# Values loaded two tokens per partition for four chunks, keys in even-odd order, and another opening order, in an attention and SwiGLU kernel

## The chip, the cores and the metric

The kernel runs on one core of a Trainium2 chip. The metric is the device time of one execution in microseconds; before and after are compared by the median of several runs. One execution of the kernel before was also recorded by the hardware profiler. Its engines are TensorE (PE, with its weight loads shown as PEld), VectorE (DVE), ScalarE (ACT), GpSimd (POOL) and SyncE (SP), which here only issues DMAs.

## What is computed

A causal attention with a window of 64 keys over 8 sequences of 576 tokens with 8 heads of 64, and behind it a feed-forward block with a gate, over all 4608 tokens. Inputs and outputs are fp32; the kernel multiplies in bf16.

```python
def _attn_ref(q, k, v):                       # each [8, 8, 576, 64]
    scores = scale * np.matmul(q, k.transpose(0, 1, 3, 2))
    rel = pos[:, None] - pos[None, :]
    mask = (rel >= 0) & (rel < window)        # window = 64
    scores = np.where(mask, scores, -1000000000.0)
    attn = np.exp(scores - np.max(scores, axis=-1, keepdims=True))
    attn = attn / (np.sum(attn, axis=-1, keepdims=True) + 1e-09)
    return np.matmul(attn, v)

def _moe_ref(x, w_gate, w_val, w_out):        # x [4608, 512], d_ff 1536
    g = x @ w_gate
    silu = g * (1.0 / (1.0 + np.exp(-g)))
    return silu * (x @ w_val) @ w_out
```

## The kernel before

The tokens are cut into 36 groups of 128 (`ORDER`): four groups for the first 512 tokens of each sequence, and four that hold the last 64 tokens of two sequences each. Two groups make a chunk (n = 0 to 17, groups 2n and 2n+1), four make a tile t of 512 tokens for the feed-forward block.

For each chunk, keys and queries are loaded as fp32 (`load`, two neighbouring tokens to a partition, so that a run in memory is 512 bytes; or `load1`, one token to a partition, runs of 256 bytes), cast to bf16 (`cast_k`) and turned so that the head dimension lies on the partitions: by TensorE against an identity and a copy out of PSUM (`turn2`), or by DMA (`turn1`). `turn2` undoes the two-token layout in its copy. `keys_before` copies the last 64 keys of a chunk to the next one's ring. Values are loaded by group, one token to a partition (`load_vg`), and `cast_v` writes them three times as bf16: `vo`, the group as it is, and the two halves to `ve`, which holds the same values shifted by 64 tokens, so that each block of 64 queries meets its 128 keys in one tile (`vL` keeps what the last 64 tokens of a sequence need).

For each group, `scores` multiplies keys and queries into two PSUM tiles. With `masked` it first writes a large negative number where the window doesn't reach (matmuls of `minus` with the identity); without, `weigh` multiplies by a mask of 0 and 1 on DVE after ACT's exponential. `products` multiplies by the values with a column of ones, `norm` divides by the sum of that column on DVE (four instructions), and `turn_x` (TensorE, then a copy on ACT) or `turn_x1` (DMA) puts the result into `xT` of its tile.

The feed-forward block of tile t is 12 `step(t, m)`, each with four matmuls for the gate, four for the values (0.86 us each four) and a tanh on ACT, then `finish` with two DVE instructions, and four `project(t, s)` of 12 matmuls. A step may be cut by columns (`step(0, 11, 0, 256)`). Weights come as 12 loads of 512 KB (`weights(s, i)`, chunk s serves steps 2s and 2s+1, i is gate or values) and six for the output (`weights_o`), each with a cast (`cast_w`, `casts_o`). `warm(n)` is n matmuls on zeros that compute nothing.

Every engine takes its instructions in the order in which the code is written (`manual_schedule`), and SP issues all DMAs in that order, each behind the release of the buffer that it fills. PSUM has four tiles (`ps_a`, tag a) for scores, products, turns and projections, and two each for gate and values (`ps_f`). `stage` holds two fp32 chunks each of keys, queries and values, `wst` six weight loads.

From line 386 to line 637 an opening is written out by hand: attention of groups 0 to 11, the 24 steps of tiles 0 and 1, the four projections of tile 0, all weights, and what the loop needs at its start. From line 641 the loop repeats a fixed pattern for each two groups, with three steps to a group; it takes up work that the opening left ready. The change touches `load_vg`, `turn2`, `cast_v`, `weigh` and `begin`, and writes the opening anew.

Of the kernel before, what the change touches and what calls it, by code (L numbers as in the profile page):

```python
# [17 lines left out]
def kernel(  # L18
# [17 lines left out]
    ORDER += [(7, i) for i in range(4)] + [(4, None), (6, None)]  # L36
    VW = 65
    KR, VR, ER, QR = 3, 5, 3, 3
    NEG = -1e30

    ctx.enter_context(tc.manual_schedule())
# [24 lines left out]

    Es = [cst.tile([P, H, 2, 64], BF16, name=f"E{i}") for i in range(ER)]

    masks = [cst.tile([P, 2, 64], BF16, name=f"mask{i}") for i in range(2)]

    minus = [cst.tile([P, P], BF16, name=f"minus{i}") for i in range(2)]
    identb = cst.tile([P, P], BF16, name="identb")
# [31 lines left out]
    def load_vg(g):  # L104

        if g % 2 == 0:
            staged["v_f", g // 2] = stage.tile([P, 2, H, D], FP32, name="v_f", tag="v_f")[:]
        for y, b, s in tokens(g):
            m = y.stop - y.start
            sp.dma_start(  # L110
                staged["v_f", g // 2][y, g % 2],
                v[b, :, s:s + m, :].rearrange("h r d -> r h d"))

    words = {}

# [41 lines left out]
    def turn2(n, nm, eng):  # L157

        x_b = words.pop((nm, n))
        o = 64 if nm == "k_f" else 0  # L160
        ring = kT[n % KR] if nm == "k_f" else qT[n % QR]
        engs = eng if isinstance(eng, tuple) else (eng,)
        m = 4 // len(engs)
        tps = []
        for i in range(len(engs)):
            tp = ps_a.tile([P, m, 2, P], BF16, name="tp", tag="a")
            for c in range(2):
                for p in range(m):
                    a = P * (m * i + p)
                    nc.tensor.transpose(tp[:, p, c], x_b[:, c, a:a + P], identb[:])  # L170
            tps.append(tp)
        for i, tp in enumerate(tps):
            y = ring[:, m * i:m * i + m, o:o + 256].rearrange("r p (x c) -> r p x c", c=2)
            copy(engs[i], y, tp[:].rearrange("r p c x -> r p x c"))

    def cast_v(g, engs):

        engs = engs if isinstance(engs, tuple) else (engs,) * 3
        x = staged["v_f", g // 2][:, g % 2]
        lo, hi = slice(0, 64), slice(64, P)  # L180
        b, i = ORDER[g]
        z = vo[g % VR]
        if i is None:
            to = (vL[hi, b], lo), (vL[hi, b + 1], hi)
        else:
            copy(engs[0], z[:, :, 0:D], x)
            to = (ve[g % VR][hi], lo), (vL[lo, b] if i == 3 else ve[(g + 1) % VR][lo], hi)
        for e, (y, a) in zip(engs[1:], to):
            if e is None:
                dve.tensor_copy(y[:, :, 0:D], z[a][:, :, 0:D])  # L190
            else:
                copy(e, y[:, :, 0:D], x[a])
# [34 lines left out]

    def weigh(g):
        E = Es[g % ER]
        mk = masks[1 if ORDER[g][1] == 0 else 0]  # L230
        ps, masked = sps.pop(g)
        for a, x in enumerate(ps):
            e = E[:, a:H:2]
            act.activation(e, x[:], AF.Exp, scale=0.125)  # L234
            if not masked:
                dve.tensor_mul(e, e, mk[:].unsqueeze(1).to_broadcast([P, 4, 2, 64]))  # L236
# [57 lines left out]
    def cast_w(s, i, eng):  # L294
        copy(eng, (wg, wv)[i][:, :, 256 * s:256 * s + 256], raw.pop((i, s))[:])
# [50 lines left out]
        for _ in range(n):  # L346
            nc.tensor.matmul(w_ps[:], wz[:, 0:P], wz[:])

    def begin():

        dve.memset(wz[:], 0.0)
# [11 lines left out]
        for a in range(2):  # L363

            y = minus[0][64 * a:64 * a + 64]
            pool.affine_select(
                out=y, in_=y, compare_op=ALU.is_ge, fill=NEG,
                base=64, pattern=[[-1, P]], channel_multiplier=1,
            )
            pool.affine_select(  # L370
                out=y, in_=y, compare_op=ALU.is_ge, fill=NEG,
                base=-1, pattern=[[1, P]], channel_multiplier=-1,
            )

        pool.tensor_copy(minus[1][:, 64:P], minus[0][:, 64:P])
# [9 lines left out]

    begin()
    load(0, k, "k_f")
    load(0, q, "q_f")
    load(1, k, "k_f")
    load_vg(0)  # L390
    cast_k(0, "q_f", (dve, act))
    cast_k(0, "k_f", pool)
    warm(11)
    turn2(0, "k_f", (act, dve))
    load(1, q, "q_f")
    warm(3)
    turn2(0, "q_f", (act, dve))
    warm(3)
    scores(0, True)
    scores(1)  # L400
    load_vg(1)
    cast_k(1, "k_f", (act, dve))
    cast_v(0, (pool, act, dve))
    load_vg(2)
    load_vg(3)
    cast_v(1, pool)
    weigh(1)
    weights(5, 0)
    weigh(0)
    warm(7)  # L410
    turn2(1, "k_f", act)
    weights(5, 1)
    cast_k(1, "q_f", dve)
    keys_before(1)
    turn2(1, "q_f", act)
    products(0)
    norm(0)
    cast_v(2, (pool, pool, act))
    warm(4)
    products(1)  # L420
    scores(2, True)
    norm(1)
    weights(0, 0)
    weights(0, 1)
    load(2, k, "k_f")
    scores(3, True)
    cast_v(3, (pool, dve, act))
    load(2, q, "q_f")
    weigh(2)
    weigh(3)  # L430
    turn_x(0)
    cast_w(5, 0, pool)
    warm(1)
    products(2)
    warm(2)
    products(3)
    norm(2)
    norm(3)
    turn_x(1)
    turn_x(2)  # L440
    load_vg(4)
    load_vg(5)
    cast_w(5, 1, pool)
    warm(2)
    step(0, 11, 0, 256)
    finish()
    cast_w(0, 0, pool)
    cast_w(0, 1, dve)
    turn_x(3)
    keys_before(2)  # L450
    step(0, 10, 0, 256)
    finish()
    cast_k(2, "k_f", (dve, pool))
    step(0, 10, 256, 256)
    finish()
    weights(4, 0)
    step(0, 0)
    weights(4, 1)
    load(3, k, "k_f")
    cast_k(2, "q_f", (act, dve))  # L460
    turn2(2, "k_f", (dve, act))
    turn2(2, "q_f", (dve, act))
    step(0, 11, 256, 256)
    finish()
    keys_before(3)
    cast_v(4, (pool, pool, act))
    scores(5, True)
    cast_v(5, (pool, dve, act))
    load(3, q, "q_f")
    weigh(5)  # L470
    scores(4, True)
    weigh(4)
    cast_w(4, 0, pool)
    finish()
    step(0, 1)
    products(5)
    load_vg(6)
    cast_w(4, 1, act)
    products(4)
    norm(5)  # L480
    weights(2, 0)
    step(0, 8)
    norm(4)
    cast_k(3, "k_f", (act, dve))
    turn_x(4)
    turn_x(5)
    finish()
    cast_k(3, "q_f", pool)
    turn2(3, "k_f", act)
    step(0, 9)  # L490
    finish()
    turn2(3, "q_f", (dve, act))
    weights(2, 1)
    load_vg(7)
    finish()
    weights(1, 0)
    step(1, 8, 0, 256)
    scores(7, True)
    finish()
    cast_w(2, 0, act)  # L500
    weights(1, 1)
    scores(6, True)
    cast_v(6, pool)
    weigh(7)
    cast_w(2, 1, dve)
    step(1, 10, 0, 256)
    load(4, q, "q_f")
    step(0, 4)
    finish()
    weigh(6)  # L510
    step(1, 4, 0, 256)
    cast_v(7, pool)
    products(7)
    finish()
    products(6)
    cast_w(1, 0, act)
    step(1, 11, 0, 256)
    load(4, k, "k_f")
    load_vg(8)
    finish()  # L520
    norm(6)
    cast_k(4, "q_f", pool)
    cast_w(1, 1, act)
    cast_k(4, "k_f", pool)
    cast_v(8, pool)
    finish()
    step(0, 5)
    step(0, 3)
    weights(3, 1)
    norm(7)  # L530
    turn_x(6)
    cast_w(3, 1, pool)
    finish()
    turn_x(7)
    turn2(4, "q_f", (dve, act))
    weights(3, 0)
    step(0, 2)
    keys_before(4)
    weights_o(4)
    finish()  # L540
    turn2(4, "k_f", act)
    finish()
    step(1, 2)
    finish()
    scores(8)
    load(5, k, "k_f")
    weigh(8)
    scores(9)
    weights_o(5)
    step(1, 8, 256, 128)  # L550
    load(5, q, "q_f")
    load_vg(9)
    cast_w(3, 0, pool)
    finish()
    cast_k(5, "k_f", pool)
    step(1, 5)
    step(0, 7)
    finish()
    finish()
    weigh(9)  # L560
    step(1, 7)
    finish()
    casts_o(5, pool)
    keys_before(5)
    turn2(5, "k_f", act)
    keys_before(6)
    step(0, 6)
    cast_k(5, "q_f", act)
    cast_v(9, pool)
    finish()  # L570
    step(1, 6)
    weights_o(2)
    finish()
    weights_o(3)
    products(8)
    casts_o(3, pool)
    products(9)
    load_vg(10)
    weights_o(0)
    step(1, 10, 256, 256)  # L580
    norm(8)
    load_vg(11)
    casts_o(2, pool)
    finish()
    casts_o(4, pool)
    cast_v(10, pool)
    step(1, 3)
    norm(9)
    turn2(5, "q_f", act)
    finish()  # L590
    turn_x(8)
    weights_o(1)
    load1(6, k, "k_f")
    casts_o(0, dve)
    casts_o(1, pool)
    step(1, 0)
    scores(10)
    scores(11)
    weigh(10)
    weigh(11)  # L600
    load1(7, k, "k_f")
    load1(7, q, "q_f")
    step(1, 9)
    cast_v(11, (dve, pool, pool))
    finish()
    turn_x(9)
    project(0, 0)
    load(6, q, "q_f")
    load_vg(12)
    project(0, 2)  # L610
    step(1, 4, 256, 256)
    products(11)
    products(10)
    cast_k(7, "k_f", (act, pool))
    finish()
    cast_k(6, "k_f", (dve, pool))
    norm(11)
    finish()
    turn1(6, "k_f")
    step(1, 1)  # L620
    cast_k(6, "q_f", act)
    norm(10)
    load_vg(14)
    cast_v(12, (act, None, None))
    keys_before(7)
    turn1(7, "k_f")
    finish()
    project(0, 1)
    turn_x(10)
    step(1, 8, 384, 128)  # L630
    load1(8, k, "k_f")
    turn_x(11)
    finish()
    project(0, 3)
    step(1, 11, 256, 256)
    load_vg(13)
    turn2(6, "q_f", (dve, act))


    dve.memset(vL[:, :, :, D:VW], 1.0)  # L640
    for w in range(8, NG, 2):
        t, s = divmod(w, 4)
        n = w // 2
# [87 lines left out]
```

The softmax here doesn't subtract the row's maximum and nothing guards it: scores larger than these inputs give would overflow.

## Time and profile before

| | us |
|---|---|
| median of 5 runs | 338.34 (337.71 to 338.69) |
| the profiled execution, its own time | 338.61 |
| its span | 336.9 |
| first matmul of the loop, from the span's start | 87.17 |
| loads of values, 256 KB each, issue to landing (median) | 5.2 |
| loads of keys and queries, 512 KB each | 7.1 |
| loads of gate and value weights, 512 KB each | 6.5 and 6.8 |

The span runs from the program's first instruction to its last; the time of an execution contains some 1.7 us around it. A row of the profile names the line of the kernel, the engine, the operation, what it writes and reads, and its shape; "idle before" is how long the engine waited ahead of it and on what.

### The profile page before, as it was taken

Reading aid. Unit: us, or ns where it says so; the run is one execution under the profiler, and the core shown is the slowest. Engines: PE = TensorE matmul, PEld = TensorE weight load, DVE = VectorE, ACT = ScalarE, POOL = GpSimd, SP = SyncE. Lnnn points to the kernel's source line nnn. Section 1 sums busy time; section 2 is a strip of 40 time slices with the busy share of each in tenths; the row PEclk is TensorE's granted clock in tenths of the full one; section 3 lists DMA queues with packets and bytes.
Section 4 is the critical chain, followed back from the end, with each engine's and each line's share of the span. In section 5 each row is a group of like instructions: output and inputs, shape, how many; then the busy total and the mean of one; then the engine's idle time right before and its main releaser. Section 6 shows DMA issues by size and latency. Waiting matters only on the chain.

```text
span 336.9 us, 7160 instructions
## 1 busy us (share of the span) xinstructions
PE 324.9 (96%) x2690; PEld 163.5 (49%) x2731; DVE 228.3 (68%) x491; ACT 151.9 (45%) x268; POOL 100.5 (30%) x148
## 2 busy tenths in 40 slices
PE   7888999999999999999999999999998999999996
PEld 3455665545544444444444444444444444444444
DVE  4667998895687767777768675867675866655520
ACT  3858876566525252525253434343433334233222
POOL 4543455751143333333333333223333110000000
DMA  7999999979978889898989689889787430211013
GB/s 204 265 312 279 309 287 324 315 161 238 190 141 174 169 163 183 166 181 174 171 179 165 149 163 177 170 173 188 140 193 124 108 65 34 63 31 31 33 47 109
DMA packets 150610, 56.83 MB, mean 169 GB/s; under 512 B 124720, under 2 KB 144560, under 8 KB 150576
## 3 DMA queue, kind: packets, MB, share of 16 engines
q1 hardware_dynamic: 150576, 56.38, 77.2%
q8 instruction: 21, 0.34, 0.4%
q14 instruction: 13, 0.11, 0.1%
HBM read 37.75 MB, written 9.44 MB: 140 GB/s over the span
## 4 chain that ended last, share of the span: by engine, by line
PE 83%; DMA 8%; DVE 4%; ACT 2%; issue 1%; SPq 1%; DVEq 0%; ACTq 0%
PE o_ps L334 26%; PE g_ps L316 25%; PE v_ps L316 24%; DMA q_f<-in_q_dram 3%; PE ao_ps L252 3%; PE s_ps L221 2%; DMA kT<-k_fb 2%; DMA v_f<-in_v_dram 2%; PE tp L170 1%; DVE sg L327 1%; ACT E L234 1%; SPq L89 1%; DVE hT L328 1%; DVE x_b L263 1%; DMA out_dram<-os__4900 1%
## 5 line engine op out<-in xcount | busy, mean ns | idle before, releaser
L316 PE MATMUL g_ps<-xT,wg 128*128 128x512 bf16 (+2 forms) x426 | 110.4, 366 | 3.7 <-DVE sg L327 1.9
L316 PE MATMUL v_ps<-xT,wv 128*128 128x512 bf16 (+1 forms) x457 | 111.6, 366 | 0.5 <-POOL wv L120 0.2
L327 DVE SCALAR_TENSOR_TENSOR sg<-th,g_ps 128x512 f32<-128x512 f32 (+1 forms) x115 | 74.9, 652 | 50.2 <-ACT th L321 50.0
L321 ACT ACTIVATE th<-g_ps 128x512 f32<-128x512 f32 (+1 forms) x115 | 65.8, 572 | 78.3 <-PE g_ps L316 75.7
L334 PE MATMUL o_ps<-wo,hT 128*128 128x512 bf16 (+2 forms) x454 | 98.4, 368 | 0.2
L328 DVE TENSOR_TENSOR hT<-sg,v_ps 128x512 bf16<-128x512 f32 (+1 forms) x115 | 75.4, 655 | 11.9 <-PE xtp L276 0.5
L316 PEld LDWEIGHTS <-wv 128*128 128x128 bf16 x460 | 44.6, 98 | 49.5 <-ACT wv L118 0.7
L334 PEld LDWEIGHTS <-hT 128*128 128x128 bf16 x456 | 43.6, 98 | 49.5
L316 PEld LDWEIGHTS <-wg 128*128 128x128 bf16 x460 | 41.9, 98 | 44.0 <-issue 2.2
L234 ACT ACTIVATE E<-s_ps 128x512 bf16<-128x512 f32 x72 | 38.6, 596 | 8.1 <-PE s_ps L221 8.0
L120 POOL CAST k_fb<-k_f 128x1024 bf16<-128x1024 f32 (+1 forms) x16 | 16.0, 1006 | 59.6 <-DMA k_f<-in_k_dram 45.1
L263 DVE TENSOR_TENSOR x_b<-ao_ps,r 128x256 bf16<-128x256 f32 x72 | 30.6, 425 | 2.5
L120 POOL CAST q_fb<-q_f 128x1024 bf16<-128x1024 f32 x13 | 13.5, 1037 | 62.2 <-DMA q_f<-in_q_dram 40.2
L236 DVE TENSOR_TENSOR E<-E,mask 128x512 bf16<-128x512 bf16 x58 | 25.3, 467 | 8.9 <-ACT E L234 8.3
L120 POOL CAST ve<-v_f 64x512 bf16<-64x512 f32 x47 | 29.3, 622 | 2.9
L120 POOL CAST vo<-v_f 128x512 bf16<-128x512 f32 x30 | 18.8, 628 | 28.9 <-DMA v_f<-in_v_dram 28.7
L262 DVE RECIPROCAL r<-ao_ps 128x4 f32<-128x4 f32 x72 | 12.5, 174 | 4.6 <-PE ao_ps L252 4.6
L252 PEld LDWEIGHTS <-E 128*64 128x64 bf16 x576 | 11.0, 110 | 7.6 <-issue 5.8
L120 POOL CAST vL<-v_f 64x512 bf16<-64x512 f32 x15 | 9.5, 631 | 11.1 <-DMA v_f<-in_v_dram 10.3
L252 PE MATMUL ao_ps<-ve,E 128*64 128x65 bf16 x256 | 11.9, 196 | 0.1
L252 PE MATMUL ao_ps<-vo,E 128*64 128x65 bf16 x256 | 11.9, 196 | 0.0
L221 PEld LDWEIGHTS <-kT 64*128 64x128 bf16 x512 | 9.1, 95 | 5.7 <-issue 3.4
(100 smaller groups left out, 144.8 us busy)
## 6 DMA issues: line engine op xcount, KB each, us to landing
v_f<-in_v_dram SPq DMA_DIRECT2D x32, 256.0 KB, 5.2
k_f<-in_k_dram SPq DMA_DIRECT2D x20, 256.0 KB, 4.2
q_f<-in_q_dram SPq DMA_DIRECT2D x18, 256.0 KB, 4.6
q_f<-in_q_dram SPq DMA_DIRECT2D x7, 512.0 KB, 7.1
k_f<-in_k_dram SPq DMA_DIRECT2D x6, 512.0 KB, 7.1
w_f<-in_moe_w_gate_dram SPq DMA_DIRECT2D x6, 512.0 KB, 6.5
w_f<-in_moe_w_val_dram SPq DMA_DIRECT2D x6, 512.0 KB, 6.8
wo_f<-in_moe_w_out_dram SPq DMA_DIRECT2D x6, 512.0 KB, 7.8
```

The costliest lines, as they stand in the source:

```text
L120: eng.tensor_copy(y, x)
L221: nc.tensor.matmul(ps[a][:, p, b], keys, qT[g // 2 % QR][y, p, o:o + 64], tile_position=(64 * a, 0), start=not masked, stop=not masked or ...
L234: act.activation(e, x[:], AF.Exp, scale=0.125)
L236: dve.tensor_mul(e, e, mk[:].unsqueeze(1).to_broadcast([P, 4, 2, 64]))
L252: nc.tensor.matmul(o_ps[64 * b:64 * b + 64, i, :], Es[g % ER][:, y, b], z[:, y, :], tile_position=(0, 64 * b),)
L262: dve.reciprocal(r[:], o_ps[:, :, D])
L263: dve.tensor_mul(xb[g][:, 256 * h:256 * h + 256].rearrange("r (y d) -> r y d", y=4), o_ps[:, :, 0:D], r[:].unsqueeze(2).to_broadcast([P, 4 ...
L316: nc.tensor.matmul(ps[:, 0:n], w[:, c, P * m:P * m + P], xT[t][:, c, c0:c0 + n], start=(c == 0), stop=(c == 3),)
L321: act.activation(th[:, 0:n], g_ps[:, 0:n], AF.Tanh, scale=0.5)
L327: dve.scalar_tensor_tensor(sg[:, 0:n], th[:, 0:n], 1.0, g_ps[:, 0:n], ALU.add, ALU.mult)
L328: dve.tensor_mul(hT[t][:, m, c0:c0 + n], sg[:, 0:n], v_ps[:, 0:n])
L334: nc.tensor.matmul(o_ps[:, a:b], hT[t][:, c, P * s:P * s + P], wo[:, c, a:b], start=(c == 0), stop=(c == 11),)
```

## The change

For the chunks 0 to 3 (`NV = 4`) values come by one load of 512 KB with two neighbouring tokens to a partition (`load_v2`) in place of two loads by group. `cast_v` then moves even and odd tokens of 32 partitions each into a block of 64: in four fp32 casts of 32 partitions to `vo`, and in two bf16 copies of 64 partitions from there to `ve` or `vL`. So within each block of 64 keys the values lie with the even tokens first and then the odd ones. The keys of these chunks are put in the same order by the copy of `turn2`, and the mask that is added by TensorE (`minus[0]`) follows that order; hence all groups up to 7 are masked on TensorE, group 1 with them. Group 28 meets keys of which half are in this order and gets a mask of its own (`mask_mixed`, written ahead of the loop). The value buffers take a tag by the parity of the chunk, one buffer each, in place of one tag with two.

The opening is in another order: groups 0 to 3 go through attention before the first step, weights are taken in the order 4, 3, 0, 2, 1, 5 in place of 5, 0, 4, 2, 1, 3, three steps are cut in place of six (one of those into three), the queries of chunks 5 and 6 come by `load1` and are turned by DMA, as are the results of groups 8 and 9, and 35 filler matmuls stand in place of 33. The loop is as before.

```diff
+    NV = 4
...
-            staged["v_f", g // 2] = stage.tile([P, 2, H, D], FP32, name="v_f", tag="v_f")[:]
+            n = g // 2
+            staged["v_f", n] = stage.tile(
+                [P, 2, H, D], FP32, name="v_f", tag=f"v_f{n % 2}", bufs=1)[:]
...
+    def load_v2(n):
+
+        x_f = stage.tile([P, H, 2, D], FP32, name="v_f", tag=f"v_f{n % 2}", bufs=1)
+        ((_, b, s),) = tokens(2 * n)
+        sp.dma_start(
+            x_f[:].rearrange("r h c d -> r h (c d)"),
+            v[b, :, s:s + 256, :].rearrange("h (r c) d -> r h (c d)", c=2),
+        )
+        staged["v_f", n] = x_f[:].rearrange("r h c d -> r c h d")
...
-            y = ring[:, m * i:m * i + m, o:o + 256].rearrange("r p (x c) -> r p x c", c=2)
-            copy(engs[i], y, tp[:].rearrange("r p c x -> r p x c"))
+            y = ring[:, m * i:m * i + m, o:o + 256]
+            x = tp[:]
+            if nm == "k_f" and n < NV:
+                y = y.rearrange("r p (w c x) -> r p c w x", w=4, c=2)
+                x = x.rearrange("r p c (w x) -> r p c w x", w=4)
+            else:
+                y = y.rearrange("r p (x c) -> r p x c", c=2)
+                x = x.rearrange("r p c x -> r p x c")
+            copy(engs[i], y, x)
...
+        before = vL[:, b] if i == 3 else ve[(g + 1) % VR]
+        if g // 2 < NV:
+            for w in range(2):
+                o = 64 * (g % 2) + 32 * w
+                for c in range(2):
+                    f = 64 * w + 32 * c
+                    copy(engs[c], z[f:f + 32, :, 0:D], x[o:o + 32, c])
+            copy(engs[2], ve[g % VR][hi, :, 0:D], z[lo, :, 0:D])
+            copy(engs[2], before[lo, :, 0:D], z[hi, :, 0:D])
+            return
...
-        mk = masks[1 if ORDER[g][1] == 0 else 0]
+        mk = masks[1 if ORDER[g][1] == 0 else 2 if ORDER[g] == (0, None) else 0]
...
+    def mask_mixed():
+        pool.tensor_copy(masks[2][64:P], masks[0][64:P])
+        pool.memset(masks[2][0:64], 1.0)
+        for c in range(2):
+            y = masks[2][32 * c:32 * c + 32]
+            pool.affine_select(
+                out=y, in_=y, compare_op=ALU.is_ge, fill=0.0,
+                base=c - 1, pattern=[[0, 2], [-1, 64]], channel_multiplier=2,
+            )
```

The start of the new opening, up to its third step, in the order in which it is written:

```diff
+    load(0, k, "k_f")
+    load_v2(0)
+    load(0, q, "q_f")
+    cast_k(0, "k_f", pool)
+    warm(11)
+    turn2(0, "k_f", dve)
+    load(1, q, "q_f")
+    load(1, k, "k_f")
+    cast_k(0, "q_f", (dve, act))
+    warm(9)
+    turn2(0, "q_f", dve)
+    cast_v(1, (pool, pool, dve))
+    keys_before(1)
+    cast_k(1, "q_f", act)
+    load_v2(1)
+    warm(3)
+    scores(0, True)
+    load(2, k, "k_f")
+    scores(1, True)
+    cast_v(0, (pool, pool, dve))
+    weigh(0)
+    weights(4, 1)
+    weigh(1)
+    cast_k(1, "k_f", pool)
+    load(2, q, "q_f")
+    warm(2)
+    turn2(1, "q_f", (act, dve))
+    weights(4, 0)
+    load_v2(2)
+    warm(2)
+    turn2(1, "k_f", (act, dve))
+    products(0)
+    weights(3, 0)
+    warm(1)
+    scores(2, True)
+    norm(0)
+    products(1)
+    norm(1)
+    cast_v(2, (pool, act, dve))
+    weigh(2)
+    warm(1)
+    turn_x(0)
+    warm(2)
+    products(2)
+    keys_before(2)
+    cast_v(3, (act, pool, pool))
+    weights(3, 1)
+    cast_k(2, "k_f", (act, dve))
+    load(3, k, "k_f")
+    cast_k(2, "q_f", pool)
+    cast_w(4, 0, pool)
+    scores(3, True)
+    cast_w(4, 1, pool)
+    load(3, q, "q_f")
+    weights(0, 0)
+    weigh(3)
+    weights(0, 1)
+    norm(2)
+    warm(3)
+    turn2(2, "k_f", (dve, act))
+    turn_x(1)
+    products(3)
+    norm(3)
+    turn_x(2)
+    keys_before(3)
+    turn2(2, "q_f", (act, dve))
+    load_v2(3)
+    turn_x(3)
+    warm(1)
+    scores(4, True)
+    scores(5, True)
+    weights(2, 0)
+    cast_v(4, (act, pool, pool))
+    cast_v(5, (dve, pool, pool))
+    weigh(5)
+    step(0, 9)
+    weigh(4)
+    cast_k(3, "q_f", pool)
+    cast_w(3, 1, act)
+    step(0, 8)
+    cast_w(3, 0, dve)
+    cast_k(3, "k_f", (act, pool))
+    weights(2, 1)
+    products(4)
+    load(4, q, "q_f")
+    load(4, k, "k_f")
+    finish()
+    step(0, 6)
+...
```

## The prediction

> **What bounds the kernel now.** I read the page's shares first, then stretches of the span, then the order of TensorE's instructions where it idles, then who ended each wait.
>
> The page, busy time and the span in 40 slices:
>
> ```profile
> span 336.9 us, 7160 instructions
> PE 324.9 (96%) x2690; PEld 163.5 (49%) x2731; DVE 228.3 (68%) x491; ACT 151.9 (45%) x268; POOL 100.5 (30%) x148
> PE   7888999999999999999999999999998999999996
> DMA  7999999979978889898989689889787430211013
> ```
>
> TensorE bounds the whole, except in the first three slices, where the DMA engines are full and TensorE is not. The stretches (PE, PEld, DVE, ACT, POOL busy, then TensorE's clock, DMA share, GB/s), and for the first twenty microseconds the same with the filler matmuls (w_ps) alone:
>
> ```profile
> 0.00:20.00 20.00, 16.39 (x213) 8.82 (x216) 10.96 (x43) 12.52 (x21) 10.20 (x26) 1.00 1.03 253
> 20.00:28.00 8.00, 6.14 (x55) 4.37 (x55) 5.03 (x13) 3.80 (x9) 3.12 (x4) 1.00 1.10 256
> 28.00:88.00 60.00, 59.31 (x611) 34.42 (x619) 49.48 (x112) 41.24 (x74) 26.57 (x35) 1.00 1.05 269
> 88.00:337.00 249.00, 243.06 (x1817) 115.90 (x1843) 162.80 (x326) 94.36 (x166) 60.64 (x85) 1.00 0.68 135
> ```
>
> ```profile
> 0.00:20.00 20.00, 9.50 (x31) 1.00 1.03 253
> ```
>
> Up to 28 us TensorE is busy 16.39 + 6.14 = 22.5 us, of which 9.5 is filler that computes nothing: real work is 13.0 of 28 us. From 28 to 88 it idles 0.7 us. The loop's first matmul stands at 87.17 us, and the loop is the same code in both kernels. So the change can win from the 15 us lost before 28, and from TensorE work that leaves the opening; nowhere else. The waits inside the loss, from the order in time of TensorE, ACT and POOL, and the chain of waits:
>
> ```profile
> 15.57 10.93 DMA q_f<-in_q_dram
> 19.59 1.04 POOL L120 CAST wv<-w_f 128x1024 bf16<-128x1024 f32 x1 [1.45 <-DMA w_f<-in_moe_w_val_dram]
> 23.82 1.02 PE L316 MATMUL g_ps<-xT,wg 128*128 128x512 bf16 x3 [0.54 <-DVE sg L327]
> 26.52 0.62 ACT L118 CAST q_fb<-q_f 128x512 bf16<-128x512 f32 x1 [1.05 <-DMA q_f<-in_q_dram]
> 27.20 0.62 PE L170 MATMUL tp<-identb,q_fb 128*128 128x128 bf16 x8 [1.05 <-ACT q_fb L118]
> ```
>
> The third queries take 10.93 us from issue to landing and end TensorE's 1.05 us wait: loads set this stage. Prices of the values' copies, from the page's groups and the order in time of DVE and POOL:
>
> ```profile
> L120 POOL CAST ve<-v_f 64x512 bf16<-64x512 f32 x47 | 29.3, 622 | 2.9
> L120 POOL CAST vo<-v_f 128x512 bf16<-128x512 f32 x30 | 18.8, 628 | 28.9 <-DMA v_f<-in_v_dram 28.7
> 81.39 0.60 DVE L190 COPY ve<-vo 64x512 bf16<-64x512 bf16 x2 [0.56 <-ACT vo L118]
> 24.51 0.87 POOL L120 CAST k_fb<-k_f 128x512 bf16<-128x512 f32 x1 [2.37 <-DMA k_f<-in_k_dram]
> ```
>
> [...] loads of 512 B runs flow at 306 GB/s (4 to 6 us), the stretch of 12 to 14 us with values in 256 B runs at 218. [...] fewer partitions save nothing; the trace agrees (622 ns for 64, 628 for 128), and I price a copy of 32 partitions at 0.62. [...] the clock here stays 1.00, and the new opening keeps 35 fillers (33 before), so I charge nothing.
>
> **The change part by part.** *Loads.* The first three 512 KB loads land at about 5.1, 6.9 and 8.75 (the casts that waited for them): 1.8 us each. Weights at 346 GB/s (16 to 20 us) take 1.5. In the new order: v0 6.9, q0 8.75, q1 10.5, k1 12.3, v1 14.1, k2 15.9, first half of weights 4 17.4, q2 19.2, other half 20.7, v2 22.5, weights 3 24.0 and 25.5, k3 27.3, q3 29.1, weights 0 30.6 and 32.1. Eight loads of 256 KB become four of 512 KB: at 218 against 306 GB/s 2.1 MB take 9.6 against 6.9 us. Later q5 and q6 lose their long runs (1.3 us back), where the DMA share falls to 0.3 for a while anyway.
>
> *Values.* A group had three fp32 casts and now has four of 32 partitions and two bf16 copies. On POOL groups 1 and 0 take 4 x 0.62 each: 6.9 to 9.4 and 9.4 to 11.9; then k1 is cast by 13.3. DVE's bf16 copy is 0.30.
>
> *The walk to the first FFN step.* q0 cast 9.4, turned 9.9, one DVE copy of 1024 columns (twice 0.61 from the row of 512) 11.2. Scores 0 and 1 to 12.2, their four exponentials at 0.55 to 13.85. That frees banks and k1 turns at 13.9 to 14.3; its copy ends at 15.0. Products 0 14.8, scores 2 15.5, norm 0 (four instructions, 1.1 us) 16.1, products 1 16.3. ACT: two value casts 16.1, exponentials 2 17.2, xT 17.7, two value casts 18.8, k2's half 19.3, exponentials 3 20.4, k2's copy 20.95, xT 1 and 2 21.95, q2's copy 22.45, xT 3 22.95. POOL stands behind ACT once: its bf16 copies for group 3 wait until 18.8 and end at 20.0, then q2 21.05, weights 4 22.1 and 23.1. TensorE: products 3 20.8, scores 4 and 5 to 23.8. So the first step starts at 23.85, where ACT and the banks end the wait, not the loads.
>
> *Against before.* At 27.66 before has groups 0 to 3, six turns, and two and a half steps at 1.73 (0.86 + 0.86 in the chain): 4.33 us. At 23.85 the new one has the same without the steps, and scores 4 and 5 more (1.0). Level point: 23.85 + 4.33 - 1.0 = 27.2, 0.5 us ahead.
>
> *After it.* TensorE runs through if its inputs are there. I walked to the tenth step: weights 3 cast by 24.6 (DVE) and 27.8 (ACT), wanted at 27.7 and 28.5; k3 and q3 cast by 30.9, wanted at 32.0; weights 0 by 31.8 and 33.3, wanted at 32.9 and 33.7; v3 on POOL 34 to 36.5, wanted at 39.1. The margins are one to three microseconds; DVE is the tightest (49.5 of 60 us before, and here all 24 steps lie behind 24 us).
>
> *Work that leaves TensorE.* Two turns of queries (8 transposes, 0.45 each) and two of x (0.22 each) go to DMA: 1.34 us. Six more DMA transposes on SP at 1.3 us (2.63 for two in the trace) stand before loads of k6 to q7, wanted only after the loop begins; SP and DMA have air there (share 0.30 at 74 to 76 us). Four fewer cut steps save DVE some 0.2 each, hidden. Group 1's masking moves from DVE (0.84) to two matmuls (0.2), among fillers. The third mask is four POOL instructions of 0.3 where POOL idles (78 to 90 us): nothing, and if POOL were late 1.2 us of POOL alone.
>
> *Sum.* 0.5 + 1.34 = 1.8. I take off 0.4 for hand-overs not in the walk (the trace shows 0.05 to 0.2 at each). Gain 1.4 on the profiled execution of 338.6: 337.2. That execution stands 0.3 above the median of 338.34, so 336.9.
>
> **Unknown costs.** [...] Load time of 512 KB: 1.5 (the rate of the weights) to 2.1 (the mean of 253 GB/s up to 20 us); at 2.1 q2 lands at 20.8, is cast by 21.8 and turns 0.3 later than in the walk, and weights 4 are still cast in time (24.3, the second half wanted at 24.7): 0.3 lost, or a little won at 1.5; taken 1.8.
>
> **Rivals.** *No change (338.3).* The chain over ACT and the banks slips by 1.4 us, and the first step starts at 25.3 and eats the gain. For it: the walk is a chain of some 25 hand-overs, 0.06 more at each is enough; against: half of them have an idle engine waiting. *Slower (339.7).* POOL's 32-partition copies cost 0.87 each because DVE is at work beside them: eight stand ahead of k1's cast, which ends 2.0 us later, and everything behind turn k1 with it; group 6's four copies then add some 0.8 ahead of products 6. 336.9 + 2.8 = 339.7. It decides from 0.80 per copy on (1.4 / 8 more than 0.62). For it: the 0.87 row; against: DVE idles 2.7 of the 6 us from 8 to 14 us[...]. *The gain is larger (335.8).* There is no hand-over loss (0.4), and before's 0.7 us of idling from 28 to 88 goes too.
>
> **How the numbers follow.** A measurement here tells about 0.2% (0.7 us) from no change. Forecast 0.45, larger 0.15, no change 0.16, slower 0.24. Forecast and larger both count as faster; of no change 0.02 falls on that side: faster 0.62, same 0.14, slower 0.24. The range runs from 335.2 (below the larger case) to 339.6, near the slower one, which leaves about 2 in 10 out; the forecast's own range is 336.2 to 337.6.
>
> **What would show it.** The first FFN matmul at about 24 us; TensorE idle under 1 us from there to the loop; the loop's first matmul near 85.7; POOL's 32-partition copies near 0.62; loads of values 1.8 us apart. Wrong would be: k1's cast after 14.5, the first step after 25.5, or waits for DVE's sg of several microseconds between 30 and 75 us.

## The result: slower, and the profile after

| | before | after |
|---|---|---|
| median, us | 338.28 (337.57 to 339.45, 47 runs) | 340.31 (338.43 to 344.32, 28 runs) |
| the profiled execution, its own time | 338.61 | 340.11 |
| its span | 336.9 | 338.4 |
| first matmul of the loop | 87.17 | 85.88 |

After takes 1.0061 times as long as before [1.0049, 1.0073]: 2.0 us slower, where 1.4 us faster was forecast. The runs of after lie wider apart than those of before.

The page of after: busy times, and the span in 40 slices of 8.46 us.

```profile
PE 326.4 (96%) x2639; PEld 161.0 (48%) x2679; DVE 228.4 (68%) x482; ACT 153.1 (45%) x266; POOL 110.1 (33%) x165
PE   7889999999799999999999999999999999999996
PEclk9999999999899999999999999999999999999999
```

The profile shows 51 matmuls fewer than before, and yet TensorE is busy for 1.5 us longer. The eleventh slice (84.6 to 93.1 us) has a 7 for TensorE and an 8 for its clock; no later slice but the last is below 9. That slice is where the loop begins. Three of the four stretches shown for before (length; PE, PEld, DVE, ACT, POOL busy; clock, DMA share, GB/s):

```profile
20.00:28.00 8.00, 7.04 (x96) 4.27 (x95) 6.34 (x12) 7.45 (x15) 6.68 (x9) 1.00 1.14 316
28.00:88.00 60.00, 59.48 (x558) 32.62 (x566) 47.69 (x105) 39.90 (x68) 29.32 (x41) 1.00 1.09 253
88.00:337.00 249.00, 243.56 (x1804) 115.64 (x1824) 161.73 (x323) 94.74 (x167) 60.13 (x85) 0.99 0.73 139
```

Up to 28 us after is better than before: TensorE is busy for 7.04 of the 8 us from 20 on (6.14 before). From 28 to 88 it idles 0.5 us. All that is lost is lost behind 88 us, in code that the change did not touch. TensorE there, in order of time (start, duration, what, and in brackets the idle time before it and who ended it):

```profile
85.88 1.03 PE L350 MATMUL g_ps<-xT,wg 128*128 128x512 bf16 x4
86.74 0.81 PE L350 MATMUL v_ps<-xT,wv 128*128 128x512 bf16 x3
87.70 0.43 PE L255 MATMUL s_ps<-qT,kT 64*128 64x64 bf16 x17
90.16 0.39 PE L255 MATMUL s_ps<-qT,kT 64*128 64x64 bf16 x15 [2.02 <-ACT os__1643 L373]
90.48 1.89 PE L350 MATMUL g_ps<-xT,wg 128*128 128x512 bf16 x4
92.16 1.89 PE L350 MATMUL v_ps<-xT,wv 128*128 128x512 bf16 x4
93.87 2.77 PE L368 MATMUL o_ps<-wo,hT 128*128 128x512 bf16 x11
```

The loop starts at 85.88, 1.29 us ahead of before. Its first step runs. The scores of the second group stop for 2.02 us for a PSUM bank that an ACT copy of a projection (os__1643) has to empty. Then the eight matmuls of the next step take 1.89 us for each four instead of 1.03: the clock has been halved (the granted clock is 0.51 from 90.4 to 93.9 us). The projection behind them starts at 93.87; in before the same projection starts at 91.31:

```profile
91.31 2.75 PE L334 MATMUL o_ps<-wo,hT 128*128 128x512 bf16 x11
```

So 1.29 us ahead have become 2.56 behind, within one round of the loop.

Why ACT was late, from the order in time of ACT, DVE and SP's queue ("SPq": start and duration of issuing a DMA):

```profile
75.37 0.60 ACT L373 ACTIVATE os__1496<-o_ps 128x512 f32<-128x512 f32 x1 [1.47 <-PE o_ps L368]
89.51 0.60 ACT L373 ACTIVATE os__1643<-o_ps 128x512 f32<-128x512 f32 x1 [5.17 <-DMA out_dram<-os__1496]
90.00 0.59 ACT L355 ACTIVATE th<-g_ps 128x512 f32<-128x512 f32 x1
90.63 0.69 DVE L361 SCALAR_TENSOR_TENSOR sg<-th,g_ps 128x512 f32<-128x512 f32 x1 [8.74 <-ACT th L355]
```

```profile
76.04 3.33 SPq L171 DMA_TRANSPOSE qT<-q_fb  x2
79.48 1.14 SPq L105 DMA_DIRECT2D k_f<-in_k_dram  x2
80.67 1.81 SPq L105 DMA_DIRECT2D q_f<-in_q_dram  x2
82.53 2.44 SPq L116 DMA_DIRECT2D v_f<-in_v_dram  x2
85.07 1.08 SPq L376 DMA_DIRECT2D out_dram<-os__1496  x1
```

`project` copies its result to one of three fp32 buffers (`os_`) and stores it from there by a DMA on SP. The result of the first projection is ready at 75.37 + 0.60 = 75.97. Its store is issued at 85.07, 9.1 us later, because two DMA transposes of chunk 6's queries and the loads of chunk 7's keys and queries and of groups 13 and 14 (six DMA instructions) stand ahead of it. SP issues without a break in that time: the four rows above the store take 8.72 of the 9.1 us. The store lands 4.34 us after its issue, as the chain of waits shows:

```profile
85.07 4.34 DMA out_dram<-os__1496
```

The fourth projection's copy needs that first buffer. It waits on ACT until 89.51. The tanh of the loop's first step stands behind it in ACT's order, DVE behind the tanh (8.74 us of idling), and TensorE behind the bank. In before, the first store went out at 74.67, as soon as its result was there (copied by 74.65), with nothing in front of it:

```profile
74.67 0.36 SPq L342 DMA_DIRECT2D out_dram<-os__1503  x1
```

The theory to test, called A in the expectations: the new opening itself gives what was forecast, and a store that is issued late behind loads on SP, together with only three result buffers, takes its gain away and more.

### The profile page after: what moved, and what is told of

The parts are those of the page before. It is cut to its first block, busy times and chain, and to the rows that moved or that the text cites. A ratio compares the mean times of both kernels' runs of the same rounds, so it can differ in the third digit from the quotient of the medians.

```text
span 338.4 us, 7083 instructions
## 1 busy us (share of the span) xinstructions
PE 326.4 (96%) x2639; PEld 161.0 (48%) x2679; DVE 228.4 (68%) x482; ACT 153.1 (45%) x266; POOL 110.1 (33%) x165
## 4 chain that ended last, share of the span: by engine, by line
PE 80%; DVE 7%; DMA 5%; ACT 3%; SPq 3%; issue 2%; DVEq 0%; ACTq 0%
PE g_ps L350 25%; PE v_ps L350 24%; PE o_ps L368 24%; PE ao_ps L286 3%; PE s_ps L255 2%; DMA q_f<-in_q_dram 2%; DVE sg L361 2%; DVE hT L362 1%; DMA out_dram<-os__1496 1%; DVE E L270 1%; SPq L171 1%; PE tp L186 1%; SPq L105 1%; DMA kT<-k_fb 1%; DVE qT L136 1%
## 5 line engine op out<-in xcount | busy, mean ns | idle before, releaser
L350 PE MATMUL g_ps<-xT,wg 128*128 128x512 bf16 (+1 forms) x415 | 110.9, 376 | 2.0 <-DVE sg L361 0.4
L355 ACT ACTIVATE th<-g_ps 128x512 f32<-128x512 f32 (+1 forms) x111 | 65.1, 586 | 75.6 <-PE g_ps L350 74.3
L350 PEld LDWEIGHTS <-wv 128*128 128x128 bf16 x444 | 43.7, 98 | 50.5 <-issue 1.1
L350 PEld LDWEIGHTS <-wg 128*128 128x128 bf16 x444 | 40.8, 98 | 44.0 <-issue 0.9
L136 POOL CAST q_fb<-q_f 128x1024 bf16<-128x1024 f32 (+1 forms) x16 | 16.2, 1014 | 67.4 <-DMA q_f<-in_q_dram 60.3
L136 POOL CAST vo<-v_f 32x512 bf16<-32x512 f32 (+1 forms) x44 | 27.6, 627 | 4.9 <-DMA v_f<-in_v_dram 3.7
L136 POOL CAST ve<-v_f 64x512 bf16<-64x512 f32 x36 | 22.2, 616 | 2.2
L255 PE MATMUL s_ps<-qT,kT 64*128 64x64 bf16 x512 | 11.3, 190 | 3.0 <-ACT os__1643 L373 2.0
```

The lines of the kernel that those rows point to most:

```text
L136: eng.tensor_copy(y, x)
L255: nc.tensor.matmul(ps[a][:, p, b], keys, qT[g // 2 % QR][y, p, o:o + 64], tile_position=(64 * a, 0), start=not masked, stop=not masked or ...
L350: nc.tensor.matmul(ps[:, 0:n], w[:, c, P * m:P * m + P], xT[t][:, c, c0:c0 + n], start=(c == 0), stop=(c == 3),)
L355: act.activation(th[:, 0:n], g_ps[:, 0:n], AF.Tanh, scale=0.5)
```

## The experiments

Each ratio is to runs of before measured beside the kernel in question.

**Five result buffers.** The smallest cure for A: the late store stays, but nobody waits for it.

```diff
-            os_ = fsb.tile([P, DM], FP32, name="os_", tag="os_")
+            os_ = fsb.tile([P, DM], FP32, name="os_", tag="os_", bufs=5)
```

> Five buffers for the projections' results (os_) in place of three, nothing else. Theory A (the fourth projection's copy waits on ACT for the first one's store, which SP issues late; the tanh of the loop's first step stands behind it; TensorE then waits 2.0 us and runs 3.4 us at half clock): the wait goes, the clock stays 1.00, 340.3 - 2.0 - 1.7 = 336.6 us. Theory B (the opening itself or the new values' layout costs the time, the wait at the loop's start only takes up slack): no change, 340 us.

Measured: 336.29 us (335.75 to 336.52), 0.9943 of before [0.9931, 0.9954]. ACT, SP and TensorE of this kernel at the start of the loop:

```profile
86.10 0.60 ACT L373 ACTIVATE os__1643<-o_ps 128x512 f32<-128x512 f32 x1 [1.74 <-PE o_ps L368]
```

```profile
85.64 1.09 SPq L376 DMA_DIRECT2D out_dram<-os__1496  x1
```

```profile
85.90 1.03 PE L350 MATMUL g_ps<-xT,wg 128*128 128x512 bf16 x4
...
88.30 1.04 PE L350 MATMUL g_ps<-xT,wg 128*128 128x512 bf16 x4
...
92.62 1.03 PE L350 MATMUL g_ps<-xT,wg 128*128 128x512 bf16 x4
```

The store is even later (85.64), but the copy now waits for TensorE's result alone and runs at 86.10, 3.4 us earlier. From the loop's first matmul to the third step at 92.62 it is 6.72 us; in after the same stretch is 85.88 to 96.48, 10.60. Of the 3.88 us of difference, 2.20 lie up to the second step (4.60 against 2.40: the wait) and 1.68 behind it (6.00 against 4.32: the halved clock).

**The store ahead of the loads.** The other end of A: three buffers as before, and `load1(7, k)`, `load1(7, q)`, `load_vg(13)` and `load_vg(14)` written behind the first projection.

```diff
-    load1(7, k, "k_f")
...
-    load1(7, q, "q_f")
...
-    load_vg(13)
...
-    load_vg(14)
     project(0, 0)
+    load1(7, k, "k_f")
+    load1(7, q, "q_f")
+    load_vg(13)
+    load_vg(14)
```

> Three buffers as before, but the loads of chunk 7's keys and queries and of the values of groups 13 and 14 are written behind the first projection, so that SP issues its store before them (about 79.5 us in place of 85.1). Theory A (order in SP's queue): the store lands before 84 us, no wait, 336.6 to 337.0 us. Theory A2 (the DMA engines themselves are too full there, whatever the order): the store still takes over 4 us and TensorE still waits 1 us or more, 339 us or more.

Measured: 336.38 us (336.15 to 336.43), ratio 0.9947 [0.9935, 0.9959]. SP's queue, then ACT:

```profile
80.20 0.52 SPq L376 DMA_DIRECT2D out_dram<-os__1487  x1
```

```profile
86.27 0.60 ACT L373 ACTIVATE os__1643<-o_ps 128x512 f32<-128x512 f32 x1 [1.79 <-issue]
```

The store goes out 4.9 us earlier and the fourth copy finds its buffer free. So the order in SP's queue decides, and not how full the DMA engines are, which the expectation had named as the other explanation. Two edits that share only this chain give the same time. Both together, with 336.3 expected if they cure one thing:

> Both cures at once, five result buffers and the store ahead of the loads of chunk 7. Theory A: they cure the same wait, so nothing adds up: 336.3 us. If the store's place also frees something else: under 335.9 us.

Measured: 336.22 us (336.02 to 337.25), ratio 0.9941 [0.9927, 0.9956]. Nothing adds up, so they cure the same loss.

**Chunk 6's queries turned by TensorE instead of DMA.** This takes the two DMA transposes (3.33 us of SP) from ahead of the store. First in the place where `turn1(6, q)` stood:

```diff
-    turn1(6, "q_f")
+    turn3(6, act)
```

(`turn3` is eight transposes into one PSUM tile and a copy on ACT.)

> Chunk 6's queries turned by TensorE and a copy on ACT in place of two DMA transposes. Theory A with the transposes as the part that holds SP: the store is issued some 3.3 us earlier (near 81.8 us), lands near 86, the wait shrinks to under 0.5 us and the clock stays full: 336.6 + 0.45 for TensorE = 337.1 us. If the loads alone hold SP: store still after 84 us, over 339.5 us.

Measured: 344.06 us (343.69 to 344.74), ratio 1.0179 [1.0165, 1.0193]: a miss. TensorE's waits by line (total, times, longest):

```profile
PE tp L205 <- POOL q_fb L136: 4.7, 1, 4.7
```

In that place TensorE stands for 4.7 us until POOL has cast those queries. The run tells nothing of SP. Put behind the third projection, where the cast is done:

> As the run with chunk 6's queries on TensorE, but the turn stands behind the third projection's place in the opening (after project(0, 2)), where the queries' cast is long done. Three result buffers. Theory A with the two DMA transposes (2.9 us of SP) as part of what holds the store: the store is issued near 82 us, the wait at the loop's start is under 0.5 us, clock full: 336.3 + 0.45 for TensorE = 336.8 us. If the transposes are not part of it: 339 us or more.

Measured: 336.77 us (336.31 to 336.91), ratio 0.9956 [0.9944, 0.9969].

```profile
82.78 1.08 SPq L385 DMA_DIRECT2D out_dram<-os__1494  x1
```

The store is issued 2.3 us earlier than in after, and that is enough. The fourth copy still waits for it a little (it runs at 87.21), but TensorE doesn't wait, and its clock stays full (1.00 from 88 us on). Moving those turns to DMA saved TensorE some 0.6 us (the loop starts at 86.51 here, at 85.90 with five buffers) and cost far more through SP. The loss needs both, the transposes and the loads ahead of the store: taking away either of them cures it, as the run with the store ahead of the loads showed for these.

**The wait filled with matmuls.** Is part of the loss the clock alone? Ten matmuls on zeros into the next step's gate tile stand between the scores of groups 12 and 13, in the loop's first round.

```diff
+        if w == 8:
+            for _ in range(10):
+                nc.tensor.matmul(g_ps[:], wz[:, 0:P], wz[:])
```

> Ten filler matmuls of 0.22 us into the next step's gate tile, between the scores of groups 12 and 13, so that TensorE is busy in the wait that remains. Theory A: the wait stays (2.0 us, now filled), the clock stays 1.00: 340.3 - 1.7 = 338.6 us. If the half clock were not due to the wait: 340.3 us and a clock of 0.995 as before.

Measured: 339.98 us (338.38 to 342.32, 10 runs), ratio 1.006 [1.0035, 1.0085]: no better than after.

```profile
88.17 2.33 PE L692 MATMUL g_ps<-wz 128*128 128x512 bf16 x10
...
92.60 0.39 PE L255 MATMUL s_ps<-qT,kT 64*128 64x64 bf16 x15 [1.97 <-ACT os__1643 L374]
92.92 1.04 PE L351 MATMUL g_ps<-xT,wg 128*128 128x512 bf16 x4
```

The clock stayed at 1.00 here (1.04 us for the step's four matmuls instead of 1.89), and eight of the ten runs kept a mean clock of 0.999 or 1.000, as against 7 of 28 in after. But in the profiled execution the awaited store was issued 1.0 us later than in after and took 5.73 us to land, at 91.84, so TensorE waited 1.97 us behind the filler too. There the gain from the clock was spent on a longer wait, and why this store took longer is not known. So filling the wait does keep the clock in most runs, as expected, while the forecast of the time missed. The price of the clock therefore rests on after itself: on its matmuls' durations (1.68 us) and, less strictly, on its runs, which have a median of 338.91 us where the mean clock was 1.000 and of 340.34 where it was 0.995. (The former may have waited less as well; there is no trace of them.) Even they are slower than before.

**The two parts apart.** The new order with five buffers, but with the values of chunks 0 to 3 loaded by group and keys and masks as before (`NV = 0`, each `load_v2(n)` two `load_vg`, no third mask). It leaves A out and asks what the layout brings.

> The new opening with five result buffers, but the values of chunks 0 to 3 as before: two loads by group in runs of 256 bytes, three casts, keys in plain order (NV = 0; the third mask is not made). If the new layout matters (2.1 MB at 218 in place of 306 GB/s, q0 lands 0.6 us later and everything behind it): 336.9 to 337.5 us. If only the order matters: 336.3 us.

Measured: 338.72 us (337.31 to 340.45, 21 runs), ratio 1.0017 [1.0005, 1.0028]: 2.4 us behind the same order with the new layout, and above both forecasts. TensorE in its opening, and stretches of two microseconds there:

```profile
22.77 0.86 PE L186 MATMUL tp<-identb,q_fb 128*128 128x128 bf16 x8 [1.46 <-POOL q_fb L136]
```

```profile
22.00:24.00 2.00, 1.23 (x13) 1.13 (x13) 1.12 (x2) 0.59 (x1) 1.54 (x2) 0.75 1.04 166
24.00:26.00 2.00, 2.00 (x36) 1.18 (x36) 0.79 (x2) 1.11 (x2) 1.94 (x3) 0.50 1.04 356
```

The third queries land late (POOL, which waits for them, begins their cast at 21.68, in after at 20.57). TensorE waits 1.46 us for the cast, its clock falls (0.75, then 0.50), and its first step starts at 26.24 instead of 24.50. The loop then starts at 87.64, 1.74 us later than with the new layout. But this trace shows one execution: 15 of the 21 runs kept a mean clock of 0.999 or 1.000, and they were no faster than the others (medians of 338.77 for the twelve at 1.000 and of 338.62 for the five at 0.995). That the layout is worth some 2.4 us to this order is shown; that the clock is part of the price is not, and where the runs at full clock lose their time no trace tells.

The other half, the old order with the new layout of values (`load_v2(n)` in the place of each pair's first `load_vg`):

> The opening of before with the new values' layout alone: one load of 512 KB in the place of the first of each chunk's two, the casts on the engines that the old opening names, group 1 masked on TensorE. If shorter loads are the gain: 337.5 us or less. If the gain needs the new order, or POOL's six copies for group 1 (3.7 us in place of 1.9) take it back: 338 to 340 us.

Measured: 345.44 us (345.02 to 346.07), ratio 1.0216 [1.0202, 1.023], worse than either theory had it. POOL and TensorE of this kernel:

```profile
10.45 4.27 POOL L136 CAST vo<-v_f 32x512 bf16<-32x512 f32 x6 [4.39 <-DMA v_f<-in_v_dram]
16.12 4.13 POOL L136 CAST vo<-v_f 32x512 bf16<-32x512 f32 x6
```

```profile
21.44 0.38 PE L310 MATMUL xtp<-identb,x_b 128*128 128x128 bf16 x4 [3.67 <-ACT E L268]
```

Twelve 32-partition copies take 8.4 us of POOL (0.70 each), ACT's bf16 copies stand behind POOL (1.84 us of waiting ahead of one) and its exponentials behind those, and TensorE waits 3.67 us. So neither half alone gains: the old order, with the copies on the engines that it names, has no room for so many small ones, and the new order needs the new loads. The gain is of the two together. Another split of the copies over the engines was not tried in the old order.

**Before, with A's parts put into it.** Five buffers alone in before, where no copy waits for a store:

> The kernel before with five result buffers. Its stores are issued early, so no wait ends on a store there: 338.1 us, no change. If more buffers are worth something by themselves: 337 us or less.

Measured: 338.21 us, ratio 0.9998 [0.999, 1.0006]. The cure does nothing where the illness is absent. Next, the illness in before: the first store held back until behind the loads of chunk 8's keys.

```diff
-    project(0, 0)
+    project(0, 0, hold=True)
...
     load1(8, k, "k_f")
+    sp.dma_start(*late.pop())
```

(`hold` puts the store into the list `late` instead of issuing it.)

> The kernel before with one thing changed: the store of its first projection is issued behind the loads of chunk 8's keys, about 86.5 us in place of 74.7, as late as in the changed kernel. Three result buffers. Theory A (a late store alone is enough, through the fourth copy on ACT): a wait of TensorE of 2 to 3 us at the loop's start, and half clock after it in most runs: 340.5 to 342.5 us. If the wait needs something else of the new opening: 338.3 us.

Measured: 338.22 us, ratio 0.9994 [0.9985, 1.0003]; inconclusive. The fourth copy started at 86.21, before the held store was even issued (86.45): it had taken another result's buffer, one freed by a store that went out on time. So the first three stores must be held together, those of `project(0, 0)`, `project(0, 2)` and `project(0, 1)`:

> The kernel before, with the stores of its first three projections all issued behind the loads of chunk 8's keys (86.5 us and after), so that no buffer of the three comes free earlier. Theory A: the fourth projection's copy on ACT, which is ready at 86.2 us, waits for the first store to land (near 90), the tanh of the loop's first step stands behind it, TensorE waits 1.5 to 3 us and then in most runs works at half clock for 3.4 us: 340 to 342.5 us. If the wait needs something else of the new opening: 338.3 us.

Measured: 338.32 us, ratio 1.0006 [0.9996, 1.0016]; a miss.

```profile
87.75 0.60 ACT L341 ACTIVATE os__1686<-o_ps 128x512 f32<-128x512 f32 x1 [3.54 <-DMA out_dram<-os__1503]
```

Now ACT does wait for the store, and the copy is 1.8 us late (it runs at 85.97 in the next kernel, which has the same stores and five buffers). But TensorE has nearly that much slack: the loop's second step starts at 89.67 instead of 89.48, 0.2 us later. The stores were not as late as planned either: the first was issued at 82.33 and not at 86.5. The companion with five buffers:

> The same late stores with five result buffers. Theory A (it is the wait for a buffer, not the late stores as such): 338.3 us as the kernel before, clock 1.00. If late stores cost by themselves (their traffic meets the loop's loads): over 339 us.

Measured: 338.14 us, ratio 0.9999 [0.999, 1.0008]. As the kernel with three buffers lost nothing either, this shows only that such late stores cost nothing by themselves. Last, the loads of group 13's values and of chunk 8's queries put ahead of the held stores as well (the latter taken from the loop's start):

> As the run of the kernel before with its first three stores held back, and two more things ahead of them in SP's queue: the values of group 13 and the queries of chunk 8 (taken from the loop's start, some 2 us of SP). In that run the fourth copy on ACT came 1.8 us late (87.75 in place of 86.0) and TensorE didn't wait, since it has two steps' banks ahead. Theory A with that slack: the copy now comes near 89.5 us, 3.5 us late, TensorE waits 1.5 to 2 us and works at half clock for 3.4 us in part of the runs: 339.5 to 342 us. If TensorE still doesn't wait, the new opening adds something of its own: 338.3 us.

Measured: 343.78 us (342.85 to 345.02), ratio 1.0159 [1.0137, 1.0181]. ACT and TensorE:

```profile
91.78 0.60 ACT L341 ACTIVATE os__1690<-o_ps 128x512 f32<-128x512 f32 x1 [7.64 <-DMA out_dram<-os__1503]
```

```profile
93.18 0.93 PE L221 MATMUL s_ps<-qT,kT 64*128 64x64 bf16 x28 [4.12 <-ACT qT L118]
94.05 1.89 PE L316 MATMUL g_ps<-xT,wg 128*128 128x512 bf16 x4
```

The same picture as in after, in the old opening: a late copy, a wait of TensorE, half clock behind it (0.50 from 92 to 96 us). (TensorE's releaser is ACT's next instruction, a copy of turned queries behind the late one.) So the old opening loses its time in the same way once its stores go out late enough (the first at 87.28). A run of this kernel with five buffers was not made, so that the two moved loads cost nothing of their own is not shown. Together the runs tell how much lateness is free: a copy 1.8 us late costs TensorE 0.2 us, 3.4 us late (after) 2.0 us, 5.8 us late 4.1 us. From these the slack is about 1.5 us, an estimate.

**More from the opening.** With the loss cured, does splitting the first queries' copy over ACT and DVE (`turn2(0, "q_f", (act, dve))`) bring its 0.3 us?

> Five result buffers, and the copy of chunk 0's queries out of PSUM (one DVE copy of 1.23 us, for which TensorE waits 0.3 to 0.9 us before the first scores) split over ACT and DVE. If the opening is a chain from q0 over ACT up to the first step: the first scores and all behind them 0.5 us earlier, 335.8 us. If the banks or later loads set the pace: 336.3 us.

Measured: 336.12 us (335.65 to 336.5), ratio 0.9932 [0.9919, 0.9944]. The first scores start at 11.01 instead of 11.09 and the first step at 24.31 instead of 24.50, but the loop at 86.12 instead of 85.90: lost on the way. It can't be told from five buffers alone. These kernels, at 336.1 to 336.3, beat both before and after.

## Why the prediction was wrong

It said 336.9 with a range from 335.2 to 339.6; after took 340.31, above the range and on the other side of before.

*Right: loads and copies.* The first queries were cast at 8.72 (forecast load 8.75), the second at 10.53 (10.5). POOL's first eight 32-partition copies and the cast of chunk 1's keys:

```profile
7.00 5.33 POOL L136 CAST vo<-v_f 32x512 bf16<-32x512 f32 x8 [0.84 <-DMA v_f<-in_v_dram]
...
12.44 1.03 POOL L136 CAST k_fb<-k_f 128x1024 bf16<-128x1024 f32 x1
```

5.33 / 8 = 0.67 us each with the step to the next, 622 ns each alone (taken 0.62, the slower rival began to decide at 0.80), and the cast ended at 13.47 (13.3).

*Right, with a small error: the walk.* The first step stood at 24.50 instead of 23.85, 0.65 us late, where 0.4 had been taken off for hand-overs. Most of it is one wait that the walk didn't have. POOL, DVE and TensorE of after:

```profile
22.00 1.04 POOL L136 CAST wg<-w_f 128x1024 bf16<-128x1024 f32 x1 [0.39 <-DMA w_f<-in_moe_w_gate_dram]
22.20 0.92 DVE L156 COPY kT<-kT 128x256 bf16<-128x256 bf16 x1
23.77 0.35 PE L255 MATMUL s_ps<-qT,kT 64*128 64x64 bf16 x12 [0.52 <-DVE qT L136]
```

DVE's copy of the last 64 keys took 0.92 us beside a cast on POOL and ended 0.08 after it; the same copy takes 0.22 us at 51.89, where POOL has no instruction. The copy of queries that TensorE waited for stood behind it. The slower rival had put such a loss on POOL's copies, from a cast of 0.87 us on POOL in before (at 24.51) beside one on DVE (24.48 to 24.91); here it fell on DVE's copy, and POOL's cast took 1.04 us, the mean of its group in after. That the cast on POOL is the cause is read from the times and was not tried.

*Right: what leaves TensorE, and no wait up to the loop.* 0.5 us of idling from 28 to 88; the loop began at 85.88 (about 85.7 was named as the sign). The opening thus gave 1.29 us of the 1.4 forecast, and the kernels with A cured show that this gain reaches the end of the program.

*Wrong: "Six more DMA transposes on SP ... stand before loads of k6 to q7, wanted only after the loop begins; SP and DMA have air there".* Two errors lie in that step. I asked who waits for the loads behind the transposes, and not what else stands in the same queue: the stores of the projections, which SP issues in order with everything else. Their buffers are three, the fourth copy needs the first again, ACT takes its work in order, and the loop's first tanh stands behind that copy. And I took the low share of the DMA engines at 74 to 76 us (0.30) for room on SP. These are two things. While the store stood in SP's queue, the DMA engines of after were less busy than those of before (stretches of after, then of before, the DMA share before the last number):

```profile
76.00:80.00 4.00, 3.95 (x52) 2.47 (x52) 3.42 (x15) 0.63 (x2) 0.00 (x0) 1.00 0.50 99
80.00:85.00 5.00, 5.00 (x30) 2.50 (x29) 1.74 (x6) 2.15 (x4) 0.81 (x1) 1.00 1.00 194
```

```profile
76.00:80.00 4.00, 3.95 (x52) 2.37 (x52) 2.10 (x8) 2.18 (x5) 1.04 (x1) 1.00 0.99 258
80.00:85.00 5.00, 5.00 (x37) 2.75 (x36) 3.39 (x10) 3.10 (x6) 0.00 (x0) 1.00 1.24 185
```

SP, however, had no room: it was issuing all that time, two of the six new transposes for 3.33 us of it. The step was priced at nothing and costs 2.20 + 1.68 = 3.88 us.

*Charged nothing: the clock.* I took the filler matmuls of the opening as enough and didn't ask for the clock at a wait later on; 1.68 us of the loss in the profiled execution are that.

*The accounts.* 1.29 us ahead at the loop's start, 2.56 behind one round later. Then 1.23 come back: before has a wait of its own for DVE's sg (1.17 us at 260.68) in a stretch of 252.73 to 262.41, 9.68 us, which is 255.52 to 263.97, 8.45 us, in after. Left: 2.56 - 1.23 = 1.3, and the spans differ by 338.4 - 336.9 = 1.5. In the kernel with five buffers the same stretch is 8.45 us as well: with it, its span is 2.1 us shorter than before's, more than the opening's 1.27. All seven profiled kernels with the old opening have this wait (0.69 to 1.18 us), and none with the new one has it there. Why it goes was not tried. No part of the prediction had it: the rival of a larger gain had named before's idle time, but that from 28 to 88 us.

*The rivals.* The time of the slower rival (339.7) lies near the measured one by accident: its cause, POOL's copies at 0.80 us or more, did not come about. No rival had the stores in it.

## What to carry to other kernels

When a step is moved or added on a queue that issues in order, list everything that is issued behind it, the stores too, and follow each one to its buffer: who takes that buffer next, on which engine, and what is queued behind that. Count the time from a result's being ready to its store's issue (9.1 us here) and the number of results in between; if buffers are as many as the results in flight, one more late issue becomes a wait of the engine that bounds the kernel (2.02 us of TensorE in after), and a spare buffer or an earlier store is the cheap cure (336.29 and 336.38 us here, from 340.31). A low share of the DMA engines doesn't tell that the engine that issues has room (0.50 from 76 to 80 us in after, while SP issued without a break). A gain in one stage should be checked against the first hand-over to the next one, as the code that loses it may be code that was not touched.

## What the runs showed of the hardware

A short wait was followed by a loss of nearly its own length again: behind the 2.02 us of waiting in after TensorE ran at a granted clock of 0.51 from 90.4 to 93.9 us, which cost 1.68 us more. Behind 1.46 us of waiting (the order alone) the clock was 0.50 from 24 to 26 us. It doesn't happen in every run: of the 28 runs of after, 7 kept a mean clock of 1.000 over the program (median 338.91 us), 16 had 0.995 (340.34) and 5 had 0.990 (342.42). In the order alone 15 of 21 kept 0.999 or 1.000, and in the kernel with the filled wait 1.97 us of waiting left it at 1.00. As an estimate from these numbers, 0.005 of the span of 338.4 us is 1.7 us, as much as the one stretch at half clock costs in the trace (1.68), and 0.990 would be two such stretches. Most of the wide range of after goes with the clock.

A store of 256 KB took 4.34 us to land behind those loads (85.07 to 89.41), and 5.73 in the kernel with the filled wait; the first store of before, which waited behind nothing, took 2.3. A cast of 32 partitions (622 ns, the mean of 22 in after) cost POOL as much as one of 128 (632 ns there, 628 in before).
